# Weight signs by ScalarE, scales from Gram products, and TensorE transposes of four tiles in an attention and MLP kernel

## The chip, the core and the metric

One core of a Trainium2 chip runs the whole program. The metric is the device time of one execution in microseconds, as the median of the runs shown. Engines are named TensorE (PE in the rows; PEld is its weight loads), VectorE (DVE), ScalarE (ACT), GpSimd (POOL) and SyncE (SP), which issues the DMA transfers.

## What is computed

Windowed attention over 8 batches, 8 heads, 576 positions of 64 values: four heads with a window of 32, four with 32 keys at a distance of 4 each. Then a normalisation, an MLP and the residual:

```python
x  = attention(q, k, v)                    # (8, 576, 512)
xn = (x - mean) / sqrt(var + 1e-6) * g
out = x + maximum(xn @ w_ch1, 0) @ w_ch2   # 512 -> 2048 -> 512, weights float64
```

The two weight matrices arrive as float64, 8 MB each, and are brought to two float16 halves (high and low) on the chip.

## The kernel before

The 4608 rows are 36 tiles of 128. A tile goes through a chain of steps with one-letter names: L and M load queries, keys and values (L125, L134), S makes scores on TensorE (L148), A takes their maximum (L174), E and F the exponentials on ScalarE (L190, L206), X transposes 32x32 blocks on VectorE (L209), V multiplies with the values (L218), v divides (L236), B and Q normalise (L255, L267), H splits the tile into high and low halves (L294) and T transposes these with DMA transfers (L311). In `values_out` the rows of the last four heads stand in another order than the tile's: four DMA copies per tile (L252, `x<-xd`) put them right.

The first six tiles are multiplied plainly: U (L331) is a product with a quarter of W1, 48 matmuls, D (L366) one with a half of W2, 24 matmuls. From tile 6 on, pairs of tiles use a Strassen scheme with seven products whose weights are sums of quarters, made once by t, k, y, P, Y, j and G (L397 to L451).

The weights come in 16 chunks of 1 MB (n = 0 to 7 for W1, 8 to 15 for W2). A float64 word is two 32-bit words, so each half of a word lies 8 bytes from the next one. The raw data of chunk n stand in one of five buffers, n % 5 of `w_sums`:

- R (`load_raw`, L585) loads the chunk.
- a (`raw_abs`, L590): ScalarE takes the upper word as a float32, makes it positive and scales it by a power of two.
- Eleven chunks: e (`raw_size`, L608) shifts that by three bits (L612) and fills in three bits of the lower word (L613), and s (`raw_signed`, L595) puts in the sign (L599), all on VectorE. The other five (1, 4, 7, 9, 10): g (`raw_sign`, L603) makes the sign as +1 or -1 on ScalarE, and q (`raw_product`, L617) multiplies on GpSimd.
- c (`raw_sums`, L627): eight matmuls of 128 columns. The stationary operand is a broadcast column (`repeated`), so the sums are column sums, over two chunks of W1 or four of W2.
- z (`scales`, L644): a power of two from their maximum, which bounds the float16 halves.
- i and l (`split_high`, `split_low`, L666, L670): the two halves, by ScalarE and VectorE.

The whole first part, to the first pair of tiles, stands in one list, `START` (L719). Each engine runs its instructions in the order of the list; so does SyncE with the loads and copies. `PAIR` (L743) is the order of the later pairs. `load_first` (L689) sets up constants and masks on GpSimd.

```python
E = mybir.EngineType
with tc.manual_schedule(engines={E.PE, E.DVE, E.Activation, E.Pool, E.SP}):
    load_first()
    for what in START:
```

Of the kernel before, what the change touches and what calls it, by code (L numbers as in the profile page):

```python
# [46 lines left out]
@with_exitstack
def attention_then_ffn(ctx: ExitStack, tc, qkv, masks, g, w1, w2, out):
# [546 lines left out]
    def raw_signed(n):  # L595
        src, dst, raw, parts = weights(n)
        for on in parts:
            hi, mi = raw[:, on, :, 1], dst[:, on].bitcast(I32)
            nc.vector.scalar_tensor_tensor(  # L599
                out=mi, in0=hi, scalar=SIGN_BIT, in1=mi, op0=ALU.bitwise_and, op1=ALU.bitwise_or  # L600
            )

    def raw_sign(n):  # L603
        for on in weights(n)[3]:
            hi = weights(n)[2][:, on, :, 1].bitcast(F32)
            nc.scalar.activation(hi, hi, AF.Sign)

    def raw_size(n):  # L608
        src, dst, raw, parts = weights(n)
        for on in parts:  # L610
            lo, mi = raw[:, on, :, 0], dst[:, on].bitcast(I32)
            nc.vector.tensor_scalar(mi, mi, scalar1=3, scalar2=None, op0=ALU.logical_shift_left)  # L612
            nc.vector.scalar_tensor_tensor(  # L613
                out=mi, in0=lo, scalar=29, in1=mi, op0=ALU.logical_shift_right, op1=ALU.bitwise_or
            )

    def raw_product(n):  # L617
        src, dst, raw, parts = weights(n)
        for on in parts:
            hi = raw[:, on, :, 1].bitcast(F32)  # L620
            nc.gpsimd.tensor_tensor(out=dst[:, on], in0=dst[:, on], in1=hi, op=ALU.mult)  # L621

    def repeated(col):

        return col.bitcast(BF16)[:, 1:2].broadcast_to([P, P])

    def raw_sums(n):  # L627
        up = weights(n)[1].bitcast(BF16).rearrange("p a (c two) -> p a c two", two=2)[:, :, :, 1]
        first_w2 = n - 2 * NKC
        if n < 2 * NKC:  # L630
            at, size, cols = n % 2, 2, [g_abs[:, c : c + 1] for c in range(CW * (n % 2), CW * (n % 2) + CW)]
        else:
            at, size, cols = first_w2 % 4, 4, [s1[first_w2 // 2][:, 1:2]] * CW
# [85 lines left out]
    START = """  # L719
        L0 R1 R0 M0 R3 R2 S0 L1 A0 a1 E0 e1 a0 F0 g1 a3 e0 c0 X0 V0 c1 s0  # L720
        a2 R4 z0 v0 q1 i0 e3 R5 e2 c2 S1 c3 l0 s2 A1 L2 M1 R6 R7 a4 E1 B0
        z1 Q0 a5 e4 c4 e5 F1 H0 T0 g4 q4 X1 V1 c5 s3 v1 S2 R8 M2 z2 i1 l1
        a6 A2 a7 E2 B1 e7 Q1 e6 s5 a8 H1 F2 X2 L3 R9 T1 e8 U0.1 o0.1 g7 i2 c6
        c7 q7 V2 v2 R10 z3 l2 s6 R11 M3 U0.0 c8 S3 A3 a9 i3 g9 a10 E3 L4 R12 B2
        e9 F3 g10 Q2 l3 e10 X3 s8 R13 U0.2 u0.2 a11 e11 U1.1 U1.0 o1.0 H2 T2 c9 q9 U0.3 V3
        v3 R14 M4 w0.2 c10 U1.2 o1.2 u1.1 c11 z4 S4 A4 s11 u0.0 w1.1 i5 i4 E4 u0.3 F4 p0.1 B3
        q10 l5 Q3 X4 w0.3 w0.0 H3 a12 i7 a14 a13 R15 T3 L5 l4 e12 l7 e13 e14 U1.3 U2.3 U2.1
        U2.0 o2.0 U2.2 V4 M5 v4 c12 U3.1 c13 a15 i6 o2.1 p2.1 U3.3 c14 p1.0 u3.1 w3.1 U3.0 S5 u2.2 w2.2
        s12 e15 c15 U3.2 u2.3 w2.3 l6 o3.0 p3.0 z5 D3.0 G1.0.2 D0.0 s13 s14 u3.2 w3.2 s15 G3.1.1 i8 l8 i9
        l9 i10 l10 A5 i11 o3.3 B4 l11 E5 u1.3 F5 k1.0.2 d0.0 D0.1 k3.1.1 Q4 j1.1.2 P1.0.1 H4 p3.3 p2.0 P3.0.1  # L730
        p1.2 P3.0.3 L6 T4 y3.1.1 X5 V5 d3.0 D3.1 y1.0.2 d0.1 j3.0.2 v5 t2.0.2 k1.1.2 y1.1.2 d3.1 M6 t2.1.2 w1.3 S6 A6
        k2.0.2 E6 L7 t1.1.1 t1.0.0 D1.0 U4.1 o4.1 F6 k3.0.2 k1.0.1 k3.0.1 k1.1.1 k2.1.2 U4.3 G1.1.3 k1.1.3 k1.0.0 k3.0.3 X6 V6 y2.0.2
        p4.1 P3.1.2 B5 Y1.0.0 P2.0.0 v6 M7 y1.1.1 P2.1.1 d1.0 D1.1 S7 U4.0 y3.0.2 G1.0.3 Q5 y3.0.3 H5 T5 L8 y1.1.3 t2.1.3
        A7 u4.3 w4.3 D2.0 B6 d1.1 Y1.0.1 P3.0.0 Y3.0.1 j1.1.0 k2.1.3 E7 F7 X7 y2.1.2 d2.0 k3.1.2 k1.1.0 u4.0 w4.0 k3.0.0 k2.0.0
        k2.1.1 Y2.1.1 Y2.0.0 P4.0.2 k1.0.3 V7 v7 y3.1.2 y2.1.3 t2.0.1 y1.0.3 D2.1 U5.3 S8 L9 M8 d2.1 A8 B7 Q6 E8 Y3.0.0
        P4.1.1 y1.1.0 U5.0 u5.0 u5.3 k2.0.1 H6 w5.0 t4.0.0 U4.2 u4.2 U5.2 k4.0.2 o5.2 Q7 F8 w4.2 X8 w5.3 t2.1.0 t2.0.3 p5.2
        Y2.0.1 P4.1.2 k2.1.0 H7 k2.0.3 D4.0 U5.1 T6 o5.1 p5.1 V8 v8 T7 M9 j3.1.0 y2.0.3 d4.0 B8 k3.1.0 D4.1 S9 L10
        A9 y2.1.0 P4.0.1 d4.1 j3.1.3 y4.0.2 U11 k4.0.0 U01 E9 k3.1.3 F9 Y4.0.0 D5.0 d5.0 X9 y3.1.0 y3.1.3 Q8 U06 k4.0.1 P4.0.3
        k4.0.3 U05 V9 Y4.0.1 Y4.0.3 v9 P4.1.3 U07 U03 U02 S10 A10 k4.1.1 U04 P4.1.0 B9 U12 D5.1 E10 F10 U16 D01
        k4.1.2 H8 U15 M10 T8 d5.1 L11 D05 U17 U13 Q9 k4.1.0 k4.1.3 X10 U14 D06 D11 D03 Y4.1.0 H9 Y4.1.1 Y4.1.2  # L740
        D12 D02 V10 v10 D07 T9 M11 N01 S11 D16 Y4.1.3 D15 D17 D13 D04 A11 D14 N05
    """.split()
    PAIR = """  # L743
        E1 L0 B0 U02 Q0 F1 X1 U11 U12 U06 H0 V1 U16 v1 U07 U03 U04 T0 U15 B1 S0 M0
        D01 U17 A0 L1 D05 Q1 D06 U13 U14 D11 H1 D02 D07 E0 F0 D12 N01 X0 D03 D16 D15 V0
        T1 v0 D04 D17 S1 M1 A1 D14 D13 N05
    """.split()

# [114 lines left out]
```

## Time and profile before

| | |
|---|---|
| median of 3 runs | 814.82 us (813.1 to 815.15) |
| span of the profiled execution | 813.2 us |
| TensorE busy | 772.9 us, 95% |
| VectorE busy | 565.4 us, 70% |
| ScalarE busy | 417.2 us, 51% |
| GpSimd busy | 443.4 us, 55% |
| bytes moved | 82.68 MB, mean 102 GB/s |

The profiled execution has its span, from its first to its last instruction, as its own time; the runs are timed without a profile. Their median lies 1.6 us above this span. A row of the groups by line reads: line, engine, operation, output and inputs, their shapes and count; busy time in all and mean ns of one; idle time just before them, and who ended it.

### The profile page before, as it was taken

The page shows a single profiled execution, that of the slowest core. Times are in us where ns is not written, and L with a number is a line of the kernel's source. Part 1 is how long each engine was busy: PE and PEld are TensorE (multiplying, and loading weights), DVE is VectorE, ACT ScalarE, POOL GpSimd, SP SyncE. Part 2 cuts the span into 40 slices and gives each one's busy share as a digit, 9 for nine tenths or more (in the row PEclk, how much of TensorE's full clock was granted, in tenths as well). Part 3 has the DMA queues.
Part 4 walks back from the last instruction along what each step waited for, and adds up shares of the span by engine and source line. Part 5 has one row for each costly group of instructions (what it writes and reads, how often), then busy time and mean ns, then how long its engine had stood idle before and what let it go on. Part 6 is the DMA issues. An engine that isn't in the chain of part 4 may idle for free.

```text
span 813.2 us, 31308 instructions
## 1 busy us (share of the span) xinstructions
PE 772.9 (95%) x13776; PEld 686.8 (84%) x13776; DVE 565.4 (70%) x1048; ACT 417.2 (51%) x712; POOL 443.4 (55%) x427
## 2 busy tenths in 40 slices
PE   2379999999999999999999999999999999999998
PEld 1268865676899999999999999999999999999997
DVE  4987889778756666666666666666666767676544
ACT  4658752654645454545454545454545454545341
POOL 4432536989983727272727272727272727272722
PEclk9869999999999999999999999999999999999999
DMA  8899803235153333434343333333333333332200
GB/s 267 287 200 260 192 30 95 79 77 105 29 96 100 76 109 74 112 71 111 72 111 72 105 77 111 72 108 75 111 72 105 76 105 78 101 82 74 34 28 27
DMA packets 144136, 82.68 MB, mean 102 GB/s; under 512 B 79680, under 2 KB 130944, under 8 KB 144000
## 3 DMA queue, kind: packets, MB, share of 16 engines
q1 hardware_dynamic: 144000, 80.69, 39.1%
q8 instruction: 108, 1.77, 0.9%
q14 instruction: 28, 0.23, 0.1%
HBM read 51.15 MB, written 9.44 MB: 75 GB/s over the span
## 4 chain that ended last, share of the span: by engine, by line
PE 89%; DVE 3%; DMA 2%; issue 1%; ACT 1%; POOL 1%; SPq 1%; POOLq 0%; DVEq 0%
PE ps_f L461 34%; PE ps_f L537 34%; PE ps_f L375 8%; PE ps_f L339 6%; PE ps_a L231 3%; PE ps_a L166 3%; DMA w_sums<-in_w 1%; DMA xT<-xl 1%; PE ps_f L639 1%; DVE w_sb L613 1%; PE ps_f L433 0%; DVE w_sb L612 0%; DMA x<-xd 0%; ACT w_sb L593 0%; POOL w_sb L621 0%
## 5 line engine op out<-in xcount | busy, mean ns | idle before, releaser
L537 PEld LDWEIGHTS <-h 128*128 128x128 f16 x2520 | 241.6, 98 | 30.7 <-issue 0.6
L471 POOL TENSOR_TENSOR h<-z,h 128x512 f16<-128x512 f32 x150 | 170.1, 1159 | 83.7 <-ACT h L470 66.4
L537 PE MATMUL ps_f<-w_sb,h 128*128 128x256 f16 x1440 | 171.8, 273 | 0.4 <-issue 0.3
L461 PE MATMUL ps_f<-xT,w_sb 128*128 128x128 f16 x2880 | 170.6, 219 | 0.0
L461 PEld LDWEIGHTS <-w_sb 128*128 128x128 f16 x2880 | 164.5, 98 | 0.8
L550 DVE SCALAR_TENSOR_TENSOR x<-ps_f,s,x 128x256 f32<-128x256 f32 x210 | 98.8, 478 | 70.3 <-PE ps_f L537 68.4
L481 ACT COPY z<-ps_f 128x512 f32<-128x512 f32 x90 | 52.5, 584 | 167.1 <-PE ps_f L461 165.6
L461 PE MATMUL ps_f<-xT,w_sums 128*128 128x128 f16 x2160 | 132.8, 219 | 0.0
L537 PE MATMUL ps_f<-w_sums,h 128*128 128x256 f16 x1080 | 127.7, 273 | 0.0
L461 PEld LDWEIGHTS <-w_sums 128*128 128x128 f16 x2160 | 124.5, 98 | 2.5
L304 POOL TENSOR_TENSOR xl<-xs,xh 128x512 f16<-128x512 f32 (+1 forms) x36 | 65.8, 1827 | 97.9 <-ACT xh L303 97.9
L470 ACT CAST h<-z 128x512 f16<-128x512 f32 x150 | 92.4, 618 | 32.2 <-DVE z L493 24.0
L188 POOL TENSOR_TENSOR sc<-sc,mx 128x512 f32<-128x512 f32 x36 | 41.4, 1150 | 118.2 <-DVE mx L187 118.2
L339 PE MATMUL ps_f<-xT,w_sb 128*128 128x128 f16 x1152 | 71.0, 225 | 2.4 <-DMA xT<-xh 1.7
L339 PEld LDWEIGHTS <-w_sb 128*128 128x128 f16 x1152 | 68.6, 101 | 4.4 <-issue 1.4
L474 DVE SCALAR_TENSOR_TENSOR h<-ps_f,h 128x512 f16<-128x512 f32 x60 | 41.5, 692 | 39.8 <-ACT h L473 39.8
L473 ACT ACTIVATE h<-ps_f 128x512 f16<-128x512 f32 x60 | 35.8, 597 | 54.5 <-DVE ps_f L485 54.1
L485 DVE TENSOR_TENSOR ps_f<-ps_f,z 128x512 f32<-128x512 f32 x60 | 41.5, 692 | 28.1 <-PE ps_f L461 28.1
L491 DVE SCALAR_TENSOR_TENSOR z<-ps_f,z 128x512 f32<-128x512 f32 x90 | 59.3, 687 | 2.4
L204 ACT ACTIVATE p<-sc 32x256 f32<-32x256 f32 x144 | 59.6, 414 | 2.6
L375 PE MATMUL ps_f<-w_sb,h 128*128 128x512 f16 x240 | 53.5, 379 | 0.0
L291 POOL TENSOR_TENSOR xs<-xs 128x256 f32<-128x256 f32 x60 | 48.7, 821 | 5.0 <-ACT xs L281 1.6
(116 smaller groups left out, 912.5 us busy)
## 6 DMA issues: line engine op xcount, KB each, us to landing
w_sums<-in_w SPq DMA_DIRECT2D x14, 1024.0 KB, 6.4
...
```

What stands on the lines that cost most here:

```text
L204: nc.scalar.activation(p32[W * to : W * (to + 1), :, :, j % 2], keys, AF.Exp, scale=1.0 / 8.0)
L291: nc.gpsimd.tensor_tensor(out=xs[:, to], in0=xs[:, x0], in1=xs[:, x1], op=op)
L304: nc.gpsimd.tensor_tensor(out=xl[:, 0:m], in0=x, in1=xh[:, 0:m], op=ALU.subtract)
L339: nc.tensor.matmul(z[:, n * P : (n + 1) * P], l, r, start=n == 0 and c == 0 and m == 0, stop=n == HG - 1 and c == NKC - 1 and m == 2,)
L375: nc.tensor.matmul(o, l, r, start=i == 0 and n == 0 and m == 0, stop=i == 1 and n == HG - 1 and m == 2,)
L461: nc.tensor.matmul(to[:, j * P : (j + 1) * P], l, r, start=start and j == 0 and k == 0 and m == 0, stop=j == HG - 1 and k == 1 and m == 2, ...
L470: nc.scalar.copy(hh, z)
L471: nc.gpsimd.tensor_tensor(out=hl, in0=z, in1=hh, op=ALU.subtract)
L481: nc.scalar.copy(z, x)
L491: nc.vector.scalar_tensor_tensor(out=to, in0=x, scalar=0.0, in1=y, op0=ALU.max, op1=op)
L537: nc.tensor.matmul(to[:, 0:KQ], l, r, start=start and j == 0 and m == 0, stop=j == HG - 1 and m == 2, skip_group_check=not start,)
L550: nc.vector.scalar_tensor_tensor(out=x, in0=ps[:, 0:KQ], scalar=state["inv", s], in1=x, op0=ALU.mult, op1=ALU.add)
```

## The change

The chunk's steps become these, for all 16 chunks. b (`raw_last`, new) shifts the lower words right by 29 bits in place on VectorE. s is now ScalarE: it reads the upper words, scales them by 2**-100 and writes them as float16, where each becomes a zero with its sign, into the upper 16 bits of the lower words. e (`raw_whole`) joins on VectorE: the positive part, shifted by three, or the lower word. g, q and the old s fall away.

In c the stationary operand is the upper 16 bits of the raw upper words, so the products are Gram products of raw and converted weights, over two chunks each; z takes their maximum, raises it to 8/9 by integer arithmetic on the bits, and for W2 adds two such parts. There are 8 steps z in place of 6. The raw buffer is so read until c.

For tiles 0 to 3, T becomes four float32 matmuls with the identity and comes before H, which splits the PSUM result on ScalarE and VectorE; and K (`values_swap`, new), a float32 matmul with a permuted identity and a ScalarE copy, takes the place of the four DMA copies. `START` is another list.

```diff
+BY_PE = 4
-        for r in range(DIL):
-            c = (r + 2) % 4
-            nc.sync.dma_start(out=x[r:P:DIL, HP * D :], in_=xd[W * c : W * (c + 1)])
-        st["x"] = x
+        st["x"], st["xd"] = x, xd
+        if t >= BY_PE:
...
+    def values_swap(t):
+        ps = bank()[:, 0 : HP * D]
+        nc.tensor.matmul(ps, swap, state[t]["xd"], start=True, stop=True)
+        nc.scalar.copy(state[t]["x"][:, HP * D :], ps)
...
     def norm_split(t):
         st = state[t]
+        if t < BY_PE:
+            z, (hi, lo) = st["xt"], (x_place(t)[:, a].rearrange("p c n -> p (c n)") for a in range(2))
+            nc.scalar.copy(hi, z)
+            nc.vector.tensor_tensor(out=lo, in0=z, in1=hi, op=ALU.subtract)
+            return
...
     def transposes(t):
         st = state[t]
+        if t < BY_PE:
+            xn = st["xs"].rearrange("p q k -> p (q k)")
+            z = st["xt"] = bank()
+            for c in range(NKC):
+                on = slice(c * P, (c + 1) * P)
+                nc.tensor.matmul(z[:, on], xn[:, on], one, start=c == 0, stop=c == NKC - 1)
+            return
...
-    def raw_signed(n):
+    def raw_last(n):
+        src, dst, raw, parts = weights(n)
+        for on in parts:
+            lo = raw[:, on, :, 0]
+            nc.vector.tensor_scalar(lo, lo, scalar1=29, scalar2=None, op0=ALU.logical_shift_right)
...
     def raw_sign(n):
+        src, dst, raw, parts = weights(n)
+        for on in parts:
+            signs = raw.bitcast(F16).rearrange("p a c (two b) -> p a c two b", two=2)[:, on, :, 0, 1]
+            nc.scalar.activation(signs, raw[:, on, :, 1].bitcast(F32), AF.Copy, scale=2.0**-100)
...
+    def raw_whole(n):
+        src, dst, raw, parts = weights(n)
+        for on in parts:
+            mi = dst[:, on].bitcast(I32)
+            nc.vector.scalar_tensor_tensor(
+                out=mi, in0=mi, scalar=3, in1=raw[:, on, :, 0], op0=ALU.logical_shift_left, op1=ALU.bitwise_or
+            )
...
     def raw_sums(n):
+        root = raw.bitcast(BF16).rearrange("p a c (two b) -> p a c two b", two=2)[:, :, :, 1, 1]
...
-                    ps[:, 0:SUMS], repeated(cols[a]), up[:, a, c : c + SUMS],
+                    ps[:, 0:SUMS], root[:, a, c : c + SUMS], up[:, a, c : c + SUMS],
...
+    def sum_of(by):
+        bound = work.tile([P, 2], F32, name="w_bound")
+        nc.vector.reduce_max(bound[:, 0:1], state["sums"][:, 0:SUMS], axis=AX.X)
+        nc.vector.tensor_scalar(
+            bound.bitcast(I32)[:, 1:2], bound.bitcast(I32)[:, 0:1], scalar1=8.0 / 9.0, scalar2=by, op0=ALU.mult, op1=ALU.add
+        )
+        return bound[:, 1:2]
...
+        for r in range(DIL):
+            c = (r + 2) % 4
+            nc.gpsimd.tensor_copy(swap[:, r:P:DIL], one[:, W * c : W * (c + 1)])
...
+        nc.vector.reduce_max(g_abs[:, NKC:], g_abs[:, 0:NKC], axis=AX.X)
+        ps = bank()[:, 0:P]
+        nc.tensor.matmul(ps, g_abs[:, NKC:].broadcast_to([P, P]), one, start=True, stop=True)
+        nc.vector.reduce_max(g_top, ps, axis=AX.X)
...
+    L0 S0 A0 R1 b1 a1 s1 e1 R0 b0 a0 s0 e0 E0 M0 F0 X0 c0 c1 z0 V0 R3 b3 a3 L1 v0 i0 l0 s3 S1 A1 K0 R5 a5 E1 F1 B0
+    M1 b5 s5 e3 Q0 R2 a2 X1 b2 s2 e5 R4 a4 V1 v1 b4 e2 s4 e4 T0 K1 L2 S2 B1 c2 c3 A2 R6 b6 H0 M2 a6 z1 c4 c5 z2 E2
+    F2 R7 X2 i1 s6 l1 a7 b7 U0.0 Q1 s7 V2 v2 L3 e6 U0.1 e7 S3 R8 a8 A3 T1 H1 u0.0 w0.0 i2 l2 c6 c7 K2 M3 R9 E3 F3
+    o0.1 B2 X3 b8 U1.0 p0.1 L4 o1.0 p1.0 U0.2 V3 U1.1 Q2 R10 M4 z3 i3 v3 K3 S4 s8 b9 s9 T2 l3 U0.3 R12 B3 L5 e8 c8
...
-        L0 R1 R0 M0 R3 R2 S0 L1 A0 a1 E0 e1 a0 F0 g1 a3 e0 c0 X0 V0 c1 s0
-        a2 R4 z0 v0 q1 i0 e3 R5 e2 c2 S1 c3 l0 s2 A1 L2 M1 R6 R7 a4 E1 B0
-        z1 Q0 a5 e4 c4 e5 F1 H0 T0 g4 q4 X1 V1 c5 s3 v1 S2 R8 M2 z2 i1 l1
-        a6 A2 a7 E2 B1 e7 Q1 e6 s5 a8 H1 F2 X2 L3 R9 T1 e8 U0.1 o0.1 g7 i2 c6
...
```

Both lists have 16 steps U and all 16 steps c ahead of the first D. Ahead of it the new list also has V, A, E, F and X of tile 5, B of tile 4, i and l of chunks 8 to 11 (steps i8 to i11 and l8 to l11, which are the first half of W2), and two steps G.

## Rows read from the trace of the kernel before

**Rows 1.** Table by stage: busy time of each engine, granted clock, DMA share, GB/s.
```profile
core 0: us, PE busy (x) PEld busy (x) DVE busy (x) ACT busy (x) POOL busy (x), PEclk, DMA share, GB/s
...
9.15:42.50 33.35, 12.00 (x309) 9.08 (x309) 30.17 (x58) 22.69 (x35) 11.37 (x10) 0.86 0.89 286
42.50:52.74 10.24, 7.33 (x128) 6.62 (x127) 9.47 (x15) 7.27 (x12) 3.52 (x3) 0.67 0.76 217
52.74:60.96 8.22, 6.38 (x126) 5.92 (x123) 6.51 (x15) 2.85 (x5) 3.06 (x2) 0.76 1.23 191
60.96:109.48 48.52, 45.29 (x994) 43.78 (x990) 39.85 (x66) 33.86 (x50) 18.45 (x14) 1.00 0.77 202
109.48:280.00 170.52, 170.52 (x2575) 127.76 (x2574) 127.53 (x215) 90.32 (x159) 131.72 (x116) 1.00 0.33 76
280.00:813.20 533.20, 529.41 (x9591) 492.40 (x9589) 351.88 (x682) 258.14 (x450) 268.71 (x249) 1.00 0.34 84
```

**Rows 2.** Waits of TensorE, 0 to 130 us: total, times, longest.
```profile
PE ps_f L639 <- DVE w_sb L613: 12.6, 3, 7.0
...
PE ps_a L166 <- DMA q<-in_qkv: 1.8, 1, 1.8
```

**Rows 3.** TensorE's timeline: the first two products with W1, start and duration.
```profile
42.52 4.71 PE L339 MATMUL ps_f<-xT,w_sb 128*128 128x128 f16 x47 [0.21 <-DMA xT<-xl]
...
52.74 4.75 PE L339 MATMUL ps_f<-xT,w_sb 128*128 128x128 f16 x48
```

**Rows 4.** Chain of waits, 95 to 130 us: start, duration, what.
```profile
102.10 0.45 PE ps_f L639 x8
...
105.23 0.22 PE ps_a L157 x2
105.45 0.79 PE ps_a L166 x53
...
106.80 2.68 PE ps_f L339 x48
109.48 5.18 PE ps_f L375 x24
114.66 0.86 PE ps_f L433 x4
...
126.75 0.79 PE ps_a L231 x53
```

**Rows 5.** VectorE by line and form, 9.15 to 109.48 us.
```profile
L599 DVE SCALAR_TENSOR_TENSOR w_sb<-w_sums,w_sb 128x1024 int32<-128x1024 int32 x7 | 8.8, 1261 | 0.0
...
L613 DVE SCALAR_TENSOR_TENSOR w_sums<-w_sums 128x1024 int32<-128x1024 int32 x4 | 4.9, 1225 | 0.1
L364 DVE SCALAR_TENSOR_TENSOR h<-ps_f,h 128x512 f16<-128x512 f32 x6 | 4.0, 676 | 0.0
...
L612 DVE TENSOR_SCALAR w_sums<-w_sums 128x1024 int32<-128x1024 int32 x4 | 2.7, 684 | 0.0
```

**Rows 6.** ScalarE by line and form, 9.15 to 109.48 us.
```profile
L593 ACT ACTIVATE w_sb<-w_sums 128x1024 f32<-128x1024 f32 x10 | 11.4, 1143 | 3.6 <-DMA w_sums<-in_w 3.6
L204 ACT ACTIVATE p<-sc 32x256 f32<-32x256 f32 x20 | 8.3, 414 | 0.4
L668 ACT ACTIVATE w_sb<-w_sb,gs 128x512 f16<-128x512 f32 x12 | 7.7, 707 | 0.3 <-DVE w_sb L599 0.3
L606 ACT ACTIVATE w_sums<-w_sums 128x1024 f32<-128x1024 f32 x4 | 4.7, 1163 | 0.0
```

**Rows 7.** GpSimd by line and form, 9.15 to 109.48 us.
```profile
L621 POOL TENSOR_TENSOR w_sb<-w_sb,w_sums 128x1024 f32<-128x1024 f32 x3 | 8.2, 2730 | 0.0
```

**Rows 8.** TensorE's weight loads by line and form, 9.15 to 109.48 us.
```profile
L339 PEld LDWEIGHTS <-w_sb 128*128 128x128 f16 x768 | 46.9, 103 | 3.5 <-issue 1.4 <-DMA xT<-xh 1.4 <-DVE w_sb L672 0.5
...
L166 PEld LDWEIGHTS ps_a<-k_ring,q 64*32 64x32 f32 x320 | 3.9, 122 | 5.2 <-issue 5.2
```

**Rows 9.** SyncE's timeline: issue of the fifth and of the last load of weights.
```profile
16.30 0.62 SPq L588 DMA_DIRECT2D w_sums<-in_w  x1
...
88.17 0.38 SPq L588 DMA_DIRECT2D w_sums<-in_w  x1
```

More of the change, by code (lines that the diff above doesn't have):

```diff
@@ L39 @@
 SUMS = 128
+BY_PE = 4
 NW2 = 2
-SIGN_BIT = -(2**31)
+ROOT = (0.5411 - 127 * 8 / 9) * 2**23
 T_W1 = 10
 T_W2 = 14
+START = """
+    L0 S0 A0 R1 b1 a1 s1 e1 R0 b0 a0 s0 e0 E0 M0 F0 X0 c0 c1 z0 V0 R3 b3 a3 L1 v0 i0 l0 s3 S1 A1 K0 R5 a5 E1 F1 B0
+    M1 b5 s5 e3 Q0 R2 a2 X1 b2 s2 e5 R4 a4 V1 v1 b4 e2 s4 e4 T0 K1 L2 S2 B1 c2 c3 A2 R6 b6 H0 M2 a6 z1 c4 c5 z2 E2
+    F2 R7 X2 i1 s6 l1 a7 b7 U0.0 Q1 s7 V2 v2 L3 e6 U0.1 e7 S3 R8 a8 A3 T1 H1 u0.0 w0.0 i2 l2 c6 c7 K2 M3 R9 E3 F3
+    o0.1 B2 X3 b8 U1.0 p0.1 L4 o1.0 p1.0 U0.2 V3 U1.1 Q2 R10 M4 z3 i3 v3 K3 S4 s8 b9 s9 T2 l3 U0.3 R12 B3 L5 e8 c8
+    R11 R13 A4 b12 P3.0.3 H2 b10 a10 u1.1 w1.1 U1.3 u0.3 E4 F4 U2.0 X4 V4 M5 a9 Q3 T3 u0.2 s10 a11 w0.2 v4 e9 U2.2
+    c9 R14 S5 L6 b11 s12 H3 e10 s11 e11 U3.0 o2.0 b13 u2.2 z4 c10 w0.3 R15 u1.3 A5 a12 a13 s13 c11 z5 e13 w2.2 E5 F5
+    X5 i4 l4 k3.0.3 b14 U1.2 U2.1 o1.2 a14 a15 b15 s14 P1.0.1 B4 y3.0.3 e14 V5 M6 i5 s15 e15 U2.3 u2.3 l5 o2.1 o3.0
+    p3.0 U3.3 U3.2 u3.2 U3.1 e12 p2.0 w2.3 c12 c13 i7 l7 w3.2 i6 u3.1 w3.1 z6 p1.2 c14 c15 z7 G1.0.3 i9 l6 l9 G1.0.2
+    i8 l8 i11 l11 i10 l10 w1.3 D3.0 d3.0 k1.0.3 y1.0.3 D0.0 D0.1 Q4 t2.0.3 H4 k1.0.2 o3.3 j1.1.0 k1.1.0 y1.0.2
+    t2.0.2 k2.0.2 P3.1.2 k3.1.2 d0.0 y1.1.0 T4 p3.3 D3.1 d0.1 k1.0.1 y2.0.2 v5 y3.1.2 P3.0.1 t1.0.0 S6 L7 A6 D1.1
+    d3.1 E6 F6 G1.1.3 B5 Q5 X6 t2.1.0 V6 M7 k2.0.3 v6 U4.1 k2.1.0 o4.1 y2.0.3 P4.0.2 t1.1.1 H5 T5 S7 L8 A7 E7 F7
+    P3.0.0 k3.0.0 Y3.0.0 j1.1.2 k1.1.2 D1.0 d1.0 d1.1 D2.1 y1.1.2 Y1.0.1 p4.1 X7 V7 M8 p2.1 v7 t2.0.1 k2.0.1 U4.3 S8
+    L9 k1.1.3 Y2.0.1 P4.0.1 u4.3 w4.3 y2.1.0 A8 U4.0 u4.0 B7 w4.0 B6 E8 U5.1 D2.0 j3.1.3 k3.1.3 F8 P4.1.0 X8 V8 M9
+    k1.0.0 o5.1 p5.1 t2.1.2 Y1.0.0 k2.1.2 Q6 d2.0 y2.1.2 k1.1.1 d2.1 U5.0 y1.1.3 H6 Q7 t2.1.3 v8 k2.1.3 y2.1.3
+    P2.0.0 j3.0.2 U5.2 U5.3 U4.2 T6 H7 u5.0 w5.0 k2.0.0 S9 L10 o5.2 Y2.0.0 u5.3 A9 B8 k3.0.2 y1.1.1 P2.1.1 u4.2 w4.2
+    D4.0 j3.1.0 E9 F9 p5.2 y3.1.3 w5.3 X9 Q8 D4.1 T7 d4.0 V9 P4.0.3 M10 U01 k4.0.3 Y4.0.3 d4.1 t4.0.0 k3.1.0 k3.0.1
+    y3.1.0 y3.0.2 Y3.0.1 U11 P4.1.2 H8 k4.0.1 D5.1 k4.1.2 v9 S10 A10 B9 U02 k4.0.2 y4.0.2 Q9 E10 F10 X10 L11 Y4.1.2
+    Y4.0.1 D5.0 k4.0.0 Y4.0.0 D01 H9 k4.1.0 k2.1.1 Y4.1.0 V10 Y2.1.1 M11 U06 d5.0 d5.1 U16 U05 U07 v10 U03 U04 U12
+    U15 U17 D05 D06 P4.1.3 U13 U14 G3.1.1 k3.1.1 y3.1.1 k4.1.3 D03 T8 D11 D12 N01 D07 D15 D16 P4.1.1 k4.1.1 Y4.1.1
+    Y4.1.3 T9 S11 A11 D17 D02 N05 D04 D14 D13
@@ L47, in attention_then_ffn @@
+""".split()
+PAIR = """
+    E1 L0 B0 U02 Q0 F1 X1 U11 U12 U06 H0 V1 U16 v1 U07 U03 U04 T0 U15 B1 S0 M0
+    D01 U17 A0 L1 D05 Q1 D06 U13 U14 D11 H1 D02 D07 E0 F0 D12 N01 X0 D03 D16 D15 V0
+    T1 v0 D04 D17 S1 M1 A1 D14 D13 N05
+""".split()
 @with_exitstack
@@ L63, in attention_then_ffn @@
     one = const.tile([P, P], F32, name="one")
+    swap = const.tile([P, P], F32, name="swap")
     plus, minus = (ident[:, i].bitcast(F16) for i in (1, 2))
@@ L101, in f32_tile, with pow2_of @@
         return halves_tile(True).bitcast(F32).rearrange("p a g n -> p (a g n)")
-    def pow2_of(bound, top, squared, name):
+    def pow2_of(bound, top, name):
         at = 2.0**23
-        e = (189 if squared else 253) + top
+        e = 253 + top
         k = work.tile([P, 2], I32, name="sc_k")
         nc.vector.tensor_scalar(
-            k[:, 0:1], bound.bitcast(I32), scalar1=24 if squared else 23, scalar2=23,
+            k[:, 0:1], bound.bitcast(I32), scalar1=23, scalar2=23,
             op0=ALU.logical_shift_right, op1=ALU.logical_shift_left,
@@ L249, in values_out @@
             )
-        for r in range(DIL):
-            c = (r + 2) % 4
-            nc.sync.dma_start(out=x[r:P:DIL, HP * D :], in_=xd[W * c : W * (c + 1)])
-        st["x"] = x
+        st["x"], st["xd"] = x, xd
+        if t >= BY_PE:
+            for r in range(DIL):
+                c = (r + 2) % 4
+                nc.sync.dma_start(out=x[r:P:DIL, HP * D :], in_=xd[W * c : W * (c + 1)])
+    def values_swap(t):
+        ps = bank()[:, 0 : HP * D]
+        nc.tensor.matmul(ps, swap, state[t]["xd"], start=True, stop=True)
+        nc.scalar.copy(state[t]["x"][:, HP * D :], ps)
     def norm_stats(t):
@@ L567, in down @@
             store(t0 + (n == 4), slice(0, DM))
-    g_abs = const.tile([P, NKC], F32, name="g_abs")
+    g_abs = const.tile([P, NKC + 1], F32, name="g_abs")
+    g_top = const.tile([P, 1], F32, name="g_top")
     s1, s12 = {}, {}
@@ L593, in raw_abs @@
             nc.scalar.activation(dst[:, on], raw[:, on, :, 1].bitcast(F32), AF.Abs, scale=2.0**-112)
-    def raw_signed(n):
+    def raw_last(n):
         src, dst, raw, parts = weights(n)
         for on in parts:
[L598 to L601, printed above, removed]
+            lo = raw[:, on, :, 0]
+            nc.vector.tensor_scalar(lo, lo, scalar1=29, scalar2=None, op0=ALU.logical_shift_right)
@@ L603, in raw_sign @@
     def raw_sign(n):
[L604 to L608, printed above, removed]
         src, dst, raw, parts = weights(n)
         for on in parts:
[L611 to L615, printed above, removed]
@@ L617, in raw_product @@
-    def raw_product(n):
+            signs = raw.bitcast(F16).rearrange("p a c (two b) -> p a c two b", two=2)[:, on, :, 0, 1]
+            nc.scalar.activation(signs, raw[:, on, :, 1].bitcast(F32), AF.Copy, scale=2.0**-100)
+    def raw_whole(n):
         src, dst, raw, parts = weights(n)
         for on in parts:
[L620 to L625, printed above, removed]
+            mi = dst[:, on].bitcast(I32)
+            nc.vector.scalar_tensor_tensor(
+                out=mi, in0=mi, scalar=3, in1=raw[:, on, :, 0], op0=ALU.logical_shift_left, op1=ALU.bitwise_or
+            )
@@ L627, in raw_sums @@
     def raw_sums(n):
[L628 to L633, printed above, removed]
+        src, dst, raw, parts = weights(n)
+        up = dst.bitcast(BF16).rearrange("p a (c two) -> p a c two", two=2)[:, :, :, 1]
@@ L634, in raw_sums @@
+        root = raw.bitcast(BF16).rearrange("p a c (two b) -> p a c two b", two=2)[:, :, :, 1, 1]
+        at = n % 2
         if at == 0:
@@ L639, in raw_sums @@
                 nc.tensor.matmul(
-                    ps[:, 0:SUMS], repeated(cols[a]), up[:, a, c : c + SUMS],
-                    start=at == 0 and a == 0 and c == 0, stop=at == size - 1 and a == CW - 1 and c == DM - SUMS,
-                )
+                    ps[:, 0:SUMS], root[:, a, c : c + SUMS], up[:, a, c : c + SUMS],
+                    start=at == 0 and a == 0 and c == 0, stop=at == 1 and a == CW - 1 and c == DM - SUMS,
+                )
+    def sum_of(by):
[5 more added lines that the diff above has]
+        return bound[:, 1:2]
     def scales(f):
-        bound = work.tile([P, 1], F32, name="w_bound")
-        nc.vector.reduce_max(bound, state["sums"][:, 0:SUMS], axis=AX.X)
         if f < NKC:
-            s = s1[f] = pow2_of(bound, T_W1, False, f"s1_{f}")
+            s = s1[f] = pow2_of(sum_of(g_top), T_W1, f"s1_{f}")
             gs = state["gs", f] = work.tile([P, NKC], F32, name="gs")
@@ L651, in scales @@
             return
-        half = f - NKC
-        s2 = pow2_of(bound, T_W2, False, f"s2_{half}")
+        half, odd = divmod(f - NKC, 2)
+        bound, by = sum_of(127.0 * 2**23 + ROOT), s1[f - NKC][:, 1:2]
+        if not odd:
+            part = state["part"] = work.tile([P, 1], F32, name="part")
+            nc.vector.tensor_scalar(part, bound, scalar1=by, scalar2=None, op0=ALU.mult)
+            return
+        nc.vector.scalar_tensor_tensor(
+            out=bound, in0=bound, scalar=by, in1=state["part"], op0=ALU.mult, op1=ALU.add
+        )
+        s2 = pow2_of(bound, T_W2, f"s2_{half}")
         state["inv", half] = s2[:, 1:2]
@@ L691, in load_first @@
         make_identity(nc, one)
+        for r in range(DIL):
+            c = (r + 2) % 4
+            nc.gpsimd.tensor_copy(swap[:, r:P:DIL], one[:, W * c : W * (c + 1)])
         for to, by in ((ident_16, 1.0), (plus, 1.0), (minus, -1.0)):
@@ L695, in load_first @@
         nc.sync.dma_start(out=mask_32, in_=masks)
-        nc.scalar.activation(g_abs, g_sb, AF.Abs)
+        nc.scalar.activation(g_abs[:, 0:NKC], g_sb, AF.Abs)
+        nc.vector.reduce_max(g_abs[:, NKC:], g_abs[:, 0:NKC], axis=AX.X)
+        ps = bank()[:, 0:P]
+        nc.tensor.matmul(ps, g_abs[:, NKC:].broadcast_to([P, P]), one, start=True, stop=True)
+        nc.vector.reduce_max(g_top, ps, axis=AX.X)
+        nc.vector.tensor_scalar(
+            g_top, g_top.bitcast(I32), scalar1=1.0, scalar2=ROOT + 0.0862 * 2**23, op0=ALU.mult, op1=ALU.add
+        )
         for n in (1, 0, 2, 3):
@@ L711, in attention_then_ffn @@
         "L": load_tile, "S": attn_scores, "A": attn_max, "E": attn_exp, "F": attn_exp_rest, "M": load_values, "X": attn_transpose, "V": attn_values,
-        "v": values_out, "B": norm_stats, "Q": norm_apply, "H": norm_split, "T": transposes,
+        "v": values_out, "B": norm_stats, "Q": norm_apply, "H": norm_split, "T": transposes, "K": values_swap,
     }
     STEPS = {
-        "R": load_raw, "a": raw_abs, "s": raw_signed, "c": raw_sums, "z": scales, "i": split_high, "l": split_low,
+        "R": load_raw, "a": raw_abs, "s": raw_sign, "b": raw_last, "e": raw_whole, "c": raw_sums, "z": scales, "i": split_high, "l": split_low,
@@ L716, in attention_then_ffn @@
         "U": up_plain, "u": up_high, "w": up_low, "D": down_plain, "d": down_out, "t": combine, "k": combine_high, "y": combine_low,
-        "P": combine_pool, "j": combine_psum, "G": combine_pe, "Y": combine_low_pool, "o": up_both, "p": up_rest, "g": raw_sign, "e": raw_size, "q": raw_product, "m": split_low_pool, "n": split_low_pe, **ATTENTION,
+        "P": combine_pool, "j": combine_psum, "G": combine_pe, "Y": combine_low_pool, "o": up_both, "p": up_rest, "m": split_low_pool, "n": split_low_pe, **ATTENTION,
@@ L718, in attention_then_ffn @@
     }
-    START = """
-        L0 R1 R0 M0 R3 R2 S0 L1 A0 a1 E0 e1 a0 F0 g1 a3 e0 c0 X0 V0 c1 s0
-        a2 R4 z0 v0 q1 i0 e3 R5 e2 c2 S1 c3 l0 s2 A1 L2 M1 R6 R7 a4 E1 B0
-        z1 Q0 a5 e4 c4 e5 F1 H0 T0 g4 q4 X1 V1 c5 s3 v1 S2 R8 M2 z2 i1 l1
-        a6 A2 a7 E2 B1 e7 Q1 e6 s5 a8 H1 F2 X2 L3 R9 T1 e8 U0.1 o0.1 g7 i2 c6
[L724 to L747, printed above, removed]
     done = set()
```

## The prediction

> **What bounds the kernel now.** I read the page first, then the table by stage, the waits of TensorE, the chain of waits, TensorE's and SyncE's timelines, and last the groups by line of each engine up to 109.5 us. The table [rows 1] shows two regimes. From 109.5 us TensorE works all the time to 280 us and for 529.4 of the 533.2 us behind that; before 109.5 us it stands or runs at half clock. So the end is TensorE's work plus what it loses in the first part. There VectorE is the full engine: 30.17 of 33.35 us from 9.15 to 42.5 us, 9.47 of the next 10.24 [rows 1], and TensorE's longest wait, 12.6 us, is for its last step of the weight conversion, L613 [rows 2]. The first two products with W1 (tile 0) begin at 42.5 and 52.7 us and take 4.7 us each, against 2.68 us later [rows 3, 4]: the granted clock was 0.67 there, which is a stretch at the lower level, 1.2 GHz, and all at 2.4 GHz from 61 us [rows 1].
>
> My mark is the first product with W2, step D3.0, at 109.5 us [rows 4]. Ahead of it both orders have the same 16 products with W1 and all 16 conversions, and behind it TensorE doesn't stand. So the end moves as the mark moves, corrected for work that goes from one side of the mark to the other.
>
> **Conversion.** Per chunk of weights, 11 of 16 lose the sign step on VectorE (L599, 1.26 us [rows 5]); 10 of these lie ahead of the mark, some 12.5 us. The other 5 lose a product on GpSimd, 2.7 us at full size [rows 7]; GpSimd is not late at the mark, so I count nothing for it. All 16 get the sign from ScalarE, 5 had that already: 11 times 1.16 us (L606 [rows 6], same input stride) is 12.8 us more there. On VectorE two steps stay two: joining (shift, or) is one instruction with two sources like L613, 1.22 us, and the other shift moves from packed words (L612, 0.68 us) to words 8 bytes apart [rows 5]. No row has a one-source instruction with that stride. Its ends are 0.68 (same operation, packed) and 1.22 us (same stride, two sources). I take 0.68, because operation and number of sources are the same. The Trainium skill, "VectorE: DVE Perf Modes", section "What auto-detection actually checks", asks of the doubled rate for 32-bit data one source, both ends in SBUF and even outer dimensions, and says nothing of the step; by it 0.68 us is right, and no run so far shows it.
>
> **Gram products.** Eight 128-column products per chunk stay eight; a chunk takes 0.45 us [rows 4]. The stationary operand is now read 8 bytes apart. Below nothing it can't go, since count and columns are the same; if the load, 0.10 us [rows 8], doubled and no longer hid, 8 of them would add up to 0.8 us a chunk, 8 us for the ten that come after the first product. I take 0: packed loads hide wholly behind a rate of 56 ns per product (2.68 us for 48), and loads of another pattern, the broadcast ones, do so too in the 0.45 us. Two extra scale steps and their extra instructions add some 2.2 us to VectorE.
>
> **Tiles 0 to 3.** Gone are 8 transposing transfers, 16 small copies of the lower half and four subtractions on GpSimd; with them SyncE's issue time ahead of the weight loads. New on TensorE: per tile four f32 products of 128 columns (T) and one of 256 (K). The nearest f32 row is the scores, 64 in 0.79 us [rows 4], eight side by side, so 0.1 us for 64 columns: four times 0.2 is 0.8 us for T, 0.4 for K. That is the low end. If the load of 128 f32 columns costs four times the 0.12 us of 32 columns [rows 8] and doesn't hide, T is 2.7 and K 0.9. I take 1.3 and 0.6, nearer the low end because loads hide in the other rows; 7.6 us in all, of which T0, K0 and K1 fall into time when TensorE waits. VectorE gets four subtractions of 0.68 us (L364 [rows 5]), ScalarE four copies, 1.6 us. The set-up adds four small copies on GpSimd ahead of the masks; the scores of tile 0 wait 1.8 us for q after the masks [rows 2], so they hide.
>
> **The order: when the first product starts.** ScalarE's queue ahead of tile 0's split holds six first passes (1.14), six signs (1.16), four scaled copies (0.71), eight quarter exponentials (0.41) [rows 6], and some 8 us of other copies and activations: 28 us less what overlaps, about 25 to 28. From 8.5 us, with 2 to 3 us for chunks that have not landed, that is 36 to 39 us; then three or four VectorE steps. VectorE's own queue to there sums to 25 us and would end near 34. So ScalarE sets it, and I put U0.0 at 40 us. A load into a raw buffer now waits for the Gram product of the chunk five before, in SyncE's order: the eighth load stands behind c2, about 36 us, and the last behind c10, about 84 us. That is near where the last load is issued now, 88.2 us [rows 9], so it costs nothing unless c10 slips. Loads R2 and R4 come behind R5, which waits for c0: the chain of tile 0 and of the first two chunks has c0 at 16 to 17 us, and SyncE now issues its fifth load at 16.3 [rows 9], so that wait costs nothing either; if it did, SyncE would hold back two chunks that TensorE needs at 36 us.
>
> **The sum to the mark.** From U0.0: 16 products of 2.68 are 42.9; four V at 0.79 are 3.2; three S at 1.0 are 3.0; ten chunks of c at 0.45 are 4.5; two combinations by TensorE at 0.86 are 1.7 [rows 4]; three T and two K are 5.1; two products at the lower clock add 4.0. Together 64.4, the mark at 104.4, and with 1.6 us of waits at 106.
>
> VectorE: its four stretches to the mark sum to 86.0 us now [rows 1]. Minus 12.5, plus 2.7 and 2.2, plus 9.7 that the order takes ahead of the mark (four split_low of W2, steps of tile 5, some lows) is 88.1. ScalarE: 66.7 now [rows 1], plus 12.8, 1.6 and 9.3 taken ahead is 90.4. A queue that sets the pace was 92% full at best [rows 1]. So VectorE reaches the mark at 9.15 + 88.1/0.92 = 104.9, ScalarE at 8.5 + 90.4/0.92 = 106.8 us. The three are within 2 us; I take 106.5, 3.0 us earlier than 109.5. The order also brings V of tile 5 and two combinations ahead of the mark, 2.5 us that are then not behind it. The end moves by -5.5 us: a span of 813.2 becomes 807.7. The median of the runs shown is 1.6 us above that span, so 809.3 us. The work behind the mark is the same in kind and number, and VectorE and GpSimd have less of it; I count no change there.
>
> **Rivals.**
> *VectorE stays the bound (slower).* If the strided shift costs 1.22 us, 16 times 0.54 adds 8.7 us to 88.1. VectorE would then fill as from 9.15 to 42.5 us, 90.5% [rows 1]: 9.15 + 96.8/0.905 = 116.1, the mark 6.6 us late, less 2.5: +4.1, 818.9 us. For it: every row with that stride is at 1.14 us or more. Against: these rows have two sources, or are ScalarE's. It turns to a loss when the shift costs above about 1.0 us. Chance 0.13.
>
> *ScalarE becomes the bound (no change).* Each sign waits for VectorE's shift, each join for the sign, in two queues in order. If ScalarE fills to only 88%, 8.5 + 90.4/0.88 = 111.2, less 2.5: -0.8, 814.0 us. For it: it goes from 66.7 to 90.4 us of work in less time. Against: its work now is only two thirds of the stretch, and it waits for other engines without harm. Chance 0.17.
>
> *The raw buffers are held too long (no change).* If c10 slips by 8 us, the last load lands near 100, its conversion and c15 end near 109, and the mark stands at 111 to 112: -0.5, 814.3 us. Chance 0.04.
>
> **How the numbers follow.** The forecast and its neighbours have 0.63; 0.03 is left for a loss that I have not named. A measurement tells 0.3%, 2.4 us: faster is below 812.4, slower above 817.3. So faster 0.63, same 0.21, slower 0.16. Low end: ScalarE's queue without a gap ends at 98.9 us, TensorE with U0.0 at 37, T of 0.8, K of 0.4 and no wait at 99.5; the better of what both allow is -12, 802.8, so I put 803. High end: 818.5, just short of the slower rival.
>
> **What would show it.** Right: U0.0 near 40 us; the mark at 105 to 108; the strided shift near 0.7 us; ScalarE over 85% busy from 20 to 100 us; no TensorE wait for xT of tiles 0 to 3. Wrong: the shift at 1.2 us with VectorE full to 110; the eight Gram products above 0.6 us a chunk at the higher clock; T above 2 us; TensorE idle between 110 and 280 us, where I count none.

## The result and the profile after: slower by 0.9%

| | before | after |
|---|---|---|
| median of 4 runs | 814.31 us | 821.98 us (820.98 to 822.18) |
| ratio, 95% interval | | 1.0089 (1.0075 to 1.0103) |
| span of the profiled execution | 813.2 us | 820.1 us |
| first product with W2 (the mark) | 109.5 us | 119.5 us |
| from the mark to the end | 703.7 us | 700.6 us |

The prediction was 809.3 us, faster; its range ended at 818.5. The mark came 10.0 us later, not 3.0 earlier. The stretch behind it is 3.1 us shorter, where the order had moved 2.5 us ahead. So the loss lies ahead of the mark.

The table by stage of the changed kernel, to its mark in the last row but one, answers to [rows 1]; columns as there.

```profile
9.15:42.50 33.35, 13.73 (x309) 10.56 (x309) 20.93 (x43) 30.80 (x37) 3.53 (x4) 1.00 0.80 256
42.50:52.74 10.24, 8.61 (x159) 8.20 (x156) 9.55 (x29) 8.00 (x12) 2.29 (x4) 0.67 0.77 265
...
60.96:119.50 58.54, 51.61 (x1063) 48.19 (x1061) 43.87 (x84) 55.00 (x68) 21.37 (x18) 0.97 0.44 142
9.15:119.50 110.35, 80.28 (x1659) 72.60 (x1660) 79.80 (x161) 102.03 (x125) 28.23 (x27) 0.95 0.61 198
119.50:280.00 160.50, 160.50 (x2424) 119.49 (x2423) 111.58 (x204) 80.90 (x141) 111.66 (x103) 1.00 0.30 77
```

VectorE and ScalarE have changed places. From 9.15 to 42.5 us VectorE was busy for 30.17 us and ScalarE for 22.69; now it is 20.93 and 30.80. ScalarE works 102.03 of the 110.35 us to the mark, and in the 40 us from 60 on it stands for only 0.9 (columns as above, ScalarE is the fourth):

```profile
60.00:80.00 20.00, 19.47 (x422) 18.52 (x420) 16.83 (x35) 19.21 (x30) 7.87 (x9) 1.00 0.70 234
80.00:100.00 20.00, 16.18 (x365) 15.14 (x362) 13.00 (x27) 19.88 (x22) 5.96 (x7) 1.00 0.60 193
```

Behind the mark TensorE has no gap up to 280 us, as before.

The groups by line of ScalarE, first 140 us (line, shapes and count, busy us and mean ns, idle before):

```profile
L655 ACT ACTIVATE w_sums<-w_sums 128x1024 f16<-128x1024 f32 x14 | 35.0, 2518 | 0.0
L643 ACT ACTIVATE w_sb<-w_sums 128x1024 f32<-128x1024 f32 x10 | 11.5, 1164 | 0.1
...
L655 ACT ACTIVATE w_sums<-w_sums 128x512 f16<-128x512 f32 x4 | 5.0, 1365 | 0.1
```

L655 is the new sign. It takes 2.52 us where L606 of before took 1.16 [rows 6]: over fourteen whole instructions and four halves some 22 us more than I had put down. The first pass, L643, reads the same words and writes float32; it takes 1.16 us, 1.14 before [rows 6].

The waits of VectorE from 9 to 118 us (waiting line, releaser, us in all, times, longest):

```profile
DVE w_sb L661 <- ACT w_sums L655: 9.8, 9, 2.1
...
DVE w_sums L661 <- ACT w_sums L655: 6.7, 3, 2.6
```

And the waits of TensorE from 0 to 150 us:

```profile
PE ps_f L675 <- DVE w_sb L661: 11.3, 3, 9.0
PE ps_a L262 <- DVE pt L244: 10.0, 4, 5.8
```

The join L661 waits 16.5 us for the sign, and the Gram products L675 wait for the join. The name in TensorE's longest wait is VectorE, as in [rows 2], but VectorE itself is being kept waiting: the view of one engine stops one step short of the cause. The chain of waits shows it: of its pieces up to 140 us, L655 holds the largest share, 24.5%.

### The profile page after: what moved, and what is told of

Its sections match the earlier page's. It is cut to its first block, busy times and chain, and to the rows that moved or that the text cites. A ratio compares the mean times of both kernels' runs of the same rounds, so it can differ in the third digit from the quotient of the medians.

```text
span 820.1 us, 31343 instructions
## 1 busy us (share of the span) xinstructions
PE 780.1 (95%) x13818; PEld 692.8 (84%) x13818; DVE 548.4 (67%) x1057; ACT 448.7 (55%) x728; POOL 422.9 (52%) x421
## 4 chain that ended last, share of the span: by engine, by line
PE 84%; ACT 11%; DVE 2%; DMA 1%; issue 1%; POOL 1%; SPq 0%; POOLq 0%; DVEq 0%
PE ps_f L510 34%; PE ps_f L586 33%; PE ps_f L424 8%; ACT w_sums L655 4%; PE ps_a L197 3%; PE ps_a L262 3%; PE ps_f L388 3%; ACT w_sb L718 1%; ACT p L235 1%; ACT w_sb L643 1%; DMA w_sums<-in_w 1%; PE ps_f L482 0%; ACT h L397 0%; ACT p L226 0%; ACT w_sums L643 0%
## 5 line engine op out<-in xcount | busy, mean ns | idle before, releaser
L346 POOL TENSOR_TENSOR xl<-xs,xh 128x512 f16<-128x512 f32 (+1 forms) x32 | 59.1, 1847 | 93.0 <-ACT xh L345 93.0
```

What stands on the lines that cost most here:

```text
L346: nc.gpsimd.tensor_tensor(out=xl[:, 0:m], in0=x, in1=xh[:, 0:m], op=ALU.subtract)
```

## The experiments

**What sets the price of the sign.** In the changed kernel eight more ScalarE instructions stand behind the sign of chunk 8 (the code is shortened: each output is named by its form):

```diff
+ activation(packed_f16,            hi, AF.Copy, scale=2.0**-100)   # L664
+ activation(f16_step_4_bytes,      hi, AF.Copy, scale=2.0**-100)   # L665
+ activation(f16_step_8_upper_half, hi, AF.Copy, scale=2.0**-100)   # L666
+ activation(f16_step_8_lower_half, hi, AF.Copy, scale=2.0**-100)   # L667
+ activation(f16_step_8_upper_half, hi, AF.Copy, scale=1.0)         # L668
+ activation(bf16_step_8,           hi, AF.Copy, scale=2.0**-100)   # L669
+ activation(f32_step_8_bytes,      hi, AF.Copy, scale=2.0**-100)   # L670
+ activation(packed_f16,            hi, AF.Copy, scale=1.0)         # L671
```

> The changed kernel with eight further ScalarE instructions behind the sign of chunk 8, all reading the same upper words of 1024 values: float16 packed, at a step of 4 bytes, at a step of 8 bytes into either half of a word, the same with scale 1 (no zeros), bfloat16 at 8 bytes, float32 at 8 bytes, float16 packed with scale 1. Theory, the step of a 16-bit write sets the price: both packed ones and the float32 one about 1.15 us, all 16-bit ones at 8 bytes about 2.5 us with either scale. Rival, the value sets it (each result underflows to a zero): all float16 ones with the small scale 2.5 us, wherever they are written, and those with scale 1 about 1.15 us. The time as a whole grows by some 10 to 18 us with the extra work and says nothing.

ScalarE by line, each instruction run once:

```profile
L668 ACT ACTIVATE w_sb<-w_sums 128x1024 f16<-128x1024 f32 x1 | 2.5, 2514 | 0.0
L667 ACT ACTIVATE w_sb<-w_sums 128x1024 f16<-128x1024 f32 x1 | 2.5, 2513 | 0.0
L666 ACT ACTIVATE w_sb<-w_sums 128x1024 f16<-128x1024 f32 x1 | 2.5, 2502 | 0.0
L669 ACT ACTIVATE w_sb<-w_sums 128x1024 bf16<-128x1024 f32 x1 | 2.5, 2467 | 0.0
L665 ACT ACTIVATE w_sb<-w_sums 128x1024 f16<-128x1024 f32 x1 | 1.4, 1384 | 0.0
L664 ACT ACTIVATE w_sb<-w_sums 128x1024 f16<-128x1024 f32 x1 | 1.2, 1186 | 0.0
L670 ACT ACTIVATE w_sb<-w_sums 128x1024 f32<-128x1024 f32 x1 | 1.1, 1123 | 0.0
L671 ACT ACTIVATE w_sb<-w_sums 128x1024 f16<-128x1024 f32 x1 | 1.1, 1108 | 0.0
```

All 16-bit writes at a step of 8 bytes take 2.5 us, in either half of the word, in either format, with zeros or without (L666 against L668). A 32-bit write at that step takes 1.12, packed 16-bit writes 1.11 to 1.19. Neither the value nor the step alone makes it: it is the 16-bit write together with the step. At 4 bytes it costs 1.38. The theory had put down no price for that, the rival 2.5 us; it opens a way out.

**The same kernel with a short sign.**

```diff
- activation(signs,                    hi, AF.Copy, scale=2.0**-100)
+ activation(raw[:, on, :, 0] as F32,  hi, AF.Copy, scale=2.0**-100)
```

> The sign is written as a float32 over the whole lower word, so the three low bits are left out and the weights are not the same; number and order of instructions are. Theory, the length of the sign instruction alone made the loss: the sign takes 1.16 us in place of 2.51, ScalarE has 21 us less, the first product with W2 starts at 105 to 109 us in place of 119.5, and the time is 806 to 813 us. Rival, the new order and the raw buffers that are held until the Gram product made it: the sign is shorter, the first product with W2 still stands at 115 to 120 us and the time at 817 to 822.

804.58 us, ratio 0.9885 (0.9861 to 0.9909). Its table by stage, to the mark at 100.7 us and behind it:

```profile
9.15:100.74 91.59, 74.72 (x1659) 67.91 (x1660) 80.00 (x163) 82.27 (x124) 27.75 (x28) 1.00 0.73 240
100.74:280.00 179.26, 179.26 (x2753) 136.39 (x2751) 121.17 (x223) 88.64 (x154) 120.67 (x109) 1.00 0.32 78
```

Its sign, by line:

```profile
L655 ACT ACTIVATE w_sums<-w_sums 128x1024 f32<-128x1024 f32 x14 | 16.1, 1161 | 0.0
```

Same order, same buffers held until the Gram product, same transposes: only the sign is shorter, by 1.36 us a chunk. ScalarE's work to the mark falls from 102.0 to 82.3 us and the mark from 119.5 to 100.7. The rival is out. Mark and time are even a little below the theory's ranges.

**That sign twice.**

```diff
  activation(raw[:, on, :, 0] as F32, hi, AF.Copy, scale=2.0**-100)
+ activation(raw[:, on, :, 0] as F32, hi, AF.Copy, scale=2.0**-100)
```

> As the kernel with the sign as a float32 over the whole lower word, but that instruction runs twice for each chunk (sign and low bits are left out as there). Theory, ScalarE's time alone counts: 2.3 us a chunk in place of 2.5, so nearly all of the loss comes back, 815 to 821 us, the first product with W2 at 114 to 119. Rival, the 16-bit writes also hold up other engines at the memory, which this does not: 804 to 810 us.

820.36 us, ratio 1.0073 (1.0059 to 1.0087). Its table by stage to 118 us, about its mark:

```profile
9.15:118.00 108.85, 78.89 (x1655) 72.11 (x1656) 79.70 (x157) 100.71 (x143) 27.42 (x27) 0.95 0.62 203
```

Its mark is at 118.9 us. 2.3 us of ScalarE made of two ordinary instructions cost nearly what the 2.5 us of one slow one cost (820.36 and 821.98 us). So the slow write harms by its length on ScalarE's queue, not by what it does at the memory.

**Signs of the even chunks by VectorE.**

```diff
+ if n % 2 == 0:   # shortened; behind the join, ScalarE's sign left out for these
+     nc.vector.scalar_tensor_tensor(out=mi, in0=hi, scalar=-(2**31), in1=mi, op0=bitwise_and, op1=bitwise_or)
```

> Signs of the even chunks are put in by VectorE, by one more instruction of 1.22 us after the join; the odd ones stay with ScalarE. Theory, ScalarE is the bound: it loses 20 us, VectorE gains 10 and has room for it, the first product with W2 starts at 106 to 112 us and the time is 807 to 815 us. Rival, VectorE takes over as the bound as before the change: 815 us or more.

815.76 us, ratio 1.0011 (0.9998 to 1.0024): faster than the changed kernel, no better than the one before. The mark is at 114.2 us. Time and mark miss the theory's ranges, if narrowly, and the time is in the rival's (815 us or more). Each holds in part: taking load from ScalarE gave 6.2 us, but VectorE then fills as well (18.90 of the 20 us from 100 to 120), and the order was made for a join that ends the chunk. Which of these two keeps the rest was not told apart.

**Transposes and copies of tiles 0 to 3 by DMA again.** `BY_PE = 0`, H and T exchanged in the list for these tiles, K empty.

> Tiles 0 to 3 are put in order and transposed by DMA transfers again, split by GpSimd, the rest as changed. Theory, ScalarE is the bound and TensorE's transposes cost little: within 4 us of the changed kernel, 818 to 826 us. Rival, the new TensorE work (four transposes and copies a tile) made the loss: 814 to 817 us.

858.44 us, ratio 1.0547 (1.0526 to 1.0569): neither. TensorE's waits, first 150 us:

```profile
PE ps_f L390 <- DMA xT<-xh: 24.2, 4, 8.1
PE ps_a L197 <- DMA q<-in_qkv: 12.3, 3, 6.0
PE ps_a L262 <- DVE pt L244: 10.9, 2, 10.2
PE ps_f L677 <- DMA w_sums<-in_w: 7.9, 1, 7.9
```

This order leaves no time for a transfer between the split and the product, and the copies stand in SyncE's queue ahead of loads of queries and weights: SyncE waits 22.7 us for what they copy. It says that the order needs the short way over TensorE, not what that way is worth in an order made for transfers.

**All new steps in the order of before,** with the sign as changed and with the short one. b stands ahead of a, s ahead of e, K behind v, H and T of tiles 0 to 3 exchanged, z where its products are ready.

> All new steps in the order of the kernel before: each shift ahead of its first pass, each sign ahead of its join, scales where their Gram products are ready. Theory, ScalarE is the bound in any order: no better than the changed kernel, 818 to 835 us. Rival, the new order made the loss: 808 to 816 us.

> The same order of the kernel before, with the sign as a float32 over the whole lower word (sign and low bits are left out). Theory, with a short sign the new steps gain in the old order too, but less than the 804.6 us in the new one: 806 to 813 us. Rival, the gain of the kernel with the short sign comes from the order alone: 814 us or more.

861.15 us (1.0574, 1.0551 to 1.0597) and 851.08 us (1.0447, 1.0433 to 1.0462). The first lies far above the ranges of both its theory and its rival. The second misses its theory and lies in the open range of its rival (814 us or more), but so far above the kernel before that it says nothing for that rival. TensorE's waits with the long sign, first 160 us:

```profile
PE ps_f L676 <- DVE w_sb L662: 32.1, 4, 13.8
PE ps_f L361 <- ACT xs L319: 22.0, 3, 11.9
PE ps_f L290 <- DVE xd L277: 6.5, 4, 2.6
```

K and T are now TensorE instructions in the middle of its queue, and what stands behind T waits until the normalisation is done. So the new steps can't simply be put into the old order; a better placing in it was not searched for. These two runs do not say what the new order is worth by itself: that it did not make the loss is shown by the kernel with the short sign, which has the same order. The 10 us between the two are the short sign's share where other waits are longer.

**The way out: 16-bit signs at a step of 4 bytes.** The shift by 29 writes packed words to a spare place, the sign goes into their upper halves, the join reads them.

```diff
- nc.vector.tensor_scalar(lo, lo, scalar1=29, ...)
+ nc.vector.tensor_scalar(low[n][:, on], raw[:, on, :, 0], scalar1=29, ...)
- signs = raw.bitcast(F16).rearrange("p a c (two b) -> p a c two b", two=2)[:, on, :, 0, 1]
+ signs = low[n].bitcast(F16).rearrange("p a (c b) -> p a c b", b=2)[:, on, :, 1]
```

In the first form the low bits of chunks 14 and 15 stand where the halves of the first chunks of W2 are split to, so these are not the same weights, and split and chunk wait for each other. The list is not quite the same either: the join of chunk 12 comes earlier in it, and here its shift and sign come later.

> The whole computation again: the shift writes the three low bits as packed words into a spare place, the sign goes as float16 into their upper halves, at a step of 4 bytes, and the join reads these; chunk 12 is taken a little later. Theory, only the step of the 16-bit writes is wrong with the change: the sign takes 1.38 us as in the probe, ScalarE has 18 us less than in the changed kernel, the first product with W2 starts at 102 to 107 us and the time is 804 to 810 us, faster than both. Rival, the writes beside VectorE's reads or the new place cost as much again: sign above 2 us, 815 us or more.

812.06 us, ratio 0.9968 (0.9956 to 0.9981); the sign took 1.36 us, as the theory had it, but TensorE was busy for only 15.27 of the 20 us from 80 to 100 at a granted clock of 0.83, where those chunks fall, and the mark is at 109.4 us: time and mark miss the theory's ranges. In the second form chunks 12, 14 and 15 have places of their own, and in the list the sign and join of chunk 15 stand ahead of i5, the join of chunk 12 as in the first form:

> The whole computation, with the sign as float16 at a step of 4 bytes into a packed spare place for the low bits. As in the run before of this kind, but chunks 12, 14 and 15 have other spare places, so that no split of W2 writes into one in use or waits for it, and chunk 12 keeps its place in the order. Theory: the sign takes 1.37 us in place of 2.51, ScalarE has 18 us less to do, three fifths to all of the 17 us between the changed kernel and the one with the short sign come back: the first product with W2 starts at 103 to 108 us, the time is 805 to 810 us, faster than both kernels. Rival: ScalarE still sets the pace at 1.37 us and the time stays at 811 to 814 us.

808.86 us, ratio 0.9935 (0.9916 to 0.9954): faster than the kernel before by 0.65%, and than the changed one by 1.5%. What the small changes of the list add to this was not told apart. Its sign, by line:

```profile
L670 ACT ACTIVATE w_sb<-w_sums 128x1024 f16<-128x1024 f32 x12 | 16.2, 1360 | 0.0
```

And the first product with W2 in TensorE's timeline, at 105.8 us:

```profile
105.83 5.34 PE L426 MATMUL ps_f<-w_sb,z 128*128 128x512 f16 x24
```

A last variant gave VectorE the signs of four chunks of that kernel (i5 is back ahead of the sign of chunk 15):

> As that one, but signs of chunks 3, 7, 11 and 15 by VectorE, behind the join: ScalarE 5.5 us less, VectorE 4.9 us more. If ScalarE still sets the pace, 1 to 4 us faster than with all signs on ScalarE; if VectorE does, 1 to 4 us slower; within 1 us if both are equally full.

809.76 us, ratio 0.9943 (0.9925 to 0.9961), within 1 us. Of the 97 us from 9.15 to about the mark ScalarE works 81.3 in place of 85.1, VectorE 87.2 in place of 81.2, and the mark stays at 106 us. So this shift gains nothing, as was expected of two engines that are about equally full.

## Why the prediction was wrong

**The step that failed** is the price of the sign in the part on the conversion: "11 times 1.16 us (L606, same input stride)". L606 writes a float32 at that step; the new instruction writes a float16. I matched engine, input and count, left out the form of the output, and set no upper end. I did bound VectorE's strided shift from both sides, and that came out at the end I had taken: 0.71 us.

```profile
L649 DVE TENSOR_SCALAR w_sums<-w_sums 128x1024 int32<-128x1024 int32 x14 | 9.9, 711 | 0.0
```

The step of 8 bytes costs next to nothing here: 0.71 us against 0.68 packed. The Trainium skill, "VectorE: DVE Perf Modes", "What auto-detection actually checks", asks for one source and both ends in SBUF and names no step for this case; the trace agrees. The rival that rested on a shift of 1.22 us (818.9 us) came within 3.1 us of the measured time by luck: its mechanism did not occur.

**The formula was right, its input wrong.** ScalarE's queue over 0.92 was to set the mark. With the measured 102.0 us that is 8.5 + 102.0/0.92 = 119.4; the mark is at 119.5, so ScalarE was about as full on the way to it as I had put down. (With the short sign it gives 98.0 against 100.7: there VectorE, 80.0 us busy, is nearly as full as ScalarE, 82.3.) The named rival "ScalarE becomes the bound" was the mechanism, but I took its loss from a poorer fill, 88% with 90.4 us of work, where the fill was right and the work was 102.0. The wait that I named with it, the join for the sign, is the 16.5 us in the table of waits.

**Other terms.** ScalarE's sum was too high even without the slow write: 90.4 us put down, 82.3 measured with the short sign. More than half of that was counted on the wrong side of the mark. Steps i8 to i11 make the second half of W2 (above it is called the first); D3.0 reads the first, which i4 to i7 make. The list has i8 to i11 ahead of D3.0, but they wait for the last scale, z7: ScalarE begins them at 100.8 us with the short sign and at 120.3 in the changed kernel, just behind the mark. Four at 1.15 us are 4.6 us. The 9.3 us that I let the order take ahead are not broken down, but come out only with these four: the other steps that it takes ahead measure some 4.8 by the groups by line. VectorE's 88.1 holds l8 to l11 in the same way; 79.8 were measured, 80.0 with the short sign. Part of the rest is that instructions overlap at their ends, so that their means add up to more than the engine is busy: in [rows 6] twelve of L668 at 0.71 us are busy for 7.7.

U0.0 was put at 40 us; it begins at 43.2 in the changed kernel and at 35.2 with the short sign, and six signs at 1.36 us are those 8 us. From there to the mark the kernel with the short sign takes 65.5 us, where the sum had 64.4 and 1.6 of waits. The 4.0 us for the lower clock did not come: 47 matmuls of U0.0 take 2.78 us there, against 4.71 for 47 in [rows 3], so the granted level was already 2.4 GHz. Of the 65.5 us TensorE works 61.7 and stands for 3.8. So the 804.6 us that the kernel takes where the sign costs what I assumed lie below my 809.3 mainly by the earlier start. One slip is without effect: the terms of the low end give -12.5 us and 802.3, not -12 and 802.8.

TensorE's new work was sized well, in part by luck. T and K in its timeline in the changed kernel, with the starts of what follows:

```profile
54.79 1.16 PE L360 MATMUL ps_f<-one,xs 128*128 128x128 f32 x8
55.78 0.64 PE L675 MATMUL ps_f<-w_sums 128*128 128x128 bf16 x8
...
58.52 0.65 PE L289 MATMUL ps_f<-xd,swap 128*128 128x256 f32 x2
59.01 0.22 PE L388 MATMUL ps_f<-xT,w_sb 128*128 128x128 f16 x1
```

T takes 1.0 us (1.3 put down), K 0.5 (0.6). The low end, 0.8 us for T, came from a misread row, here from TensorE's timeline of the kernel before:

```profile
105.38 0.86 PE L166 MATMUL ps_a<-k_ring,q 64*32 64x64 f32 x64
```

The program makes 32 float32 products for the scores of a tile, and these are its 64 matmuls in the trace. Read so, the same working gives 1.6 us as the low end, above what T takes. In the chain of the kernel with the short sign 32 Gram products take 1.90 us, 0.48 a chunk against 0.45 before: strided weight loads hide, as I took them to. The raw buffers' rival did not come: ScalarE waited 1.4 us in all for loads of weights. The wait of TensorE for xT, which I had excluded, did come, with 3.8 us. That the stretch behind the mark would only lose what was moved out of it was right.
